# A new order for the steps of a three-stage kernel, and one PSUM bank in place of two for block 0

## The chip, the cores and the metric

The kernel runs on one core of a Trainium2 chip. The metric is device time in microseconds (us). The kernel before takes 833.93 us, the median of three runs (833.71 to 834.21).

The engines are named as in the profile: PE is TensorE's matmul, PEld its weight load, DVE is VectorE, ACT is ScalarE, POOL is GpSimd, SP is SyncE, which issues most of the transfers. A suffix q (SPq) means the engine's instruction queue.

## The reference, cut to what matters

```python
kv  = einsum('bhsd,bhse->bhde', k, v)          # 4 batches, 8 heads, 576 positions, 64 wide
a   = einsum('bhsd,bhde->bhse', q, kv)
a   = a / sqrt(mean(a * a) + 1e-06) * g_norm
x   = a as (2304 tokens, 512)
xn  = x / sqrt(mean(x * x) + 1e-06) * rms_g
x   = (silu(xn @ w_gate) * (xn @ w_val)) @ w_out     # 512 -> 1536 -> 512
h   = x @ w_in2                                      # 512 -> 2048
out = where(h > 0, h, exp(min(h, 0)) - 1) @ w_out2   # 2048 -> 512
```

All in float32. The kernel keeps every operand of a product as a high and a low part and adds three matmuls for each product (high by high, high by low, low by high).

## The kernel before

The 2304 tokens are 18 tiles of 128. The tiles are five blocks: block 0 has 256 tokens, blocks 1 to 4 have 512. Block 0 is worked alone; blocks 1 and 2, and blocks 3 and 4, are pairs (`PAIRS`).

There are three stages. The attention makes the tokens and their norm and turns them to the layout of the products. Stage 0 is the gated feed-forward (12 slices of 128 hidden columns: gate weights g, value weights v, output weights o). Stage 1 is the ELU feed-forward (16 slices, weights i and p). The output of each group of slices is added up in memory by transfers with addition (`mid`, `out`), and the last group is added on chip.

For pairs of blocks, two products with four quarters each are made from seven products instead of eight (`paired` for the hidden layer, `back_halved` for some of the output products). Each of these units opens accumulators a, b and c. Accumulator a is copied out by ACT between products ("snap"), b and c are added to the copies by DVE ("total").

Block 0 goes through `plain_hidden`. For one slice of stage 0 it makes four chunks of three 128x256 matmuls for the gate, then four for the value. After the gate's last chunk ACT computes Silu of the gate (step "gate", L933), and after the value's last chunk DVE multiplies it by the value (step "gated", L937). In the kernel before, gate and value have a PSUM bank each, of kind "g" (four banks: bg0, bg1, bg2, bo4; the first two slices use "g0", bg0 to bg2). The gate's bank is free again after "gate", the value's after "gated".

Nothing of the order is written out by hand. Every step is added to a `Plan` with an engine, an estimated length, a rank, the steps it must follow, and the buffers it takes. `Plan.run` then:

- makes an order with `order()`: at each point it takes the step that can start first, and among those that can start within 0.03 us of each other on an engine the one with the lowest rank. This pass also decides which buffer each step gets.
- makes six more passes with `again()`, whose ranks are the latest start times that `latest()` derives from the pass before; the buffers stay those of the first pass.
- keeps the pass with the earliest planned end and emits the instructions in its order. Each engine runs its own instructions in that order, one behind the other, and so does SP's queue.

The ranks that are given are multiples of 100 from one unit to the next (`R`, with `LEAD` 400 and `LEAD2` 250 for the weights); inside a unit they go by single steps, and the output products stand at 50 behind their unit.

While the keys and values are summed (until the last tile's sum), `run` puts matmuls without use (`keep_warm`, L351) where the plan shows PE idle for longer than 0.375 us. They write columns 256 to 383 of the bank whose columns 0 to 255 hold the sums of keys by values. ACT copies these sums out (`keep_kv`, L378). The loads (`LOADS`) are a chain, each behind the one before it.

Of the kernel before, what the change touches and what calls it, by code (L numbers as in the profile page):

```python
# [16 lines left out]
P = 128  # L17
D = 64
G = 2
EPS = 1e-06  # L20
WARM = 16
INF_FIELD = 2.0**-96 * 1.75


class Plan:
# [199 lines left out]
BACK_HALVED = {(0, 2): 1, (0, 4): 3, (0, 6): 3, (0, 8): 3, (1, 2): 3, (1, 4): 1, (1, 6): 3, (1, 8): 1, (1, 10): 3, (1, 12): 3}  # L225
WHOLE_AFTER = 17
SEEDS = ()
SPARE = [f"{x}{f}" for f in range(2, 12) for x in "gvo"] + [f"{x}{f}" for f in range(2, 16) for x in "ip"]


@with_exitstack
def linear_attention__swiglu__elu_kernel(
# [410 lines left out]
    def half_product(unit, X, one, two, m, c):  # L643
        _, b, a, x, first = next(p for p in PRODUCTS if p[0] == m)
        if first and c == 0:
            pbank[unit, b] = bank((unit, b))
# [9 lines left out]
    def paired(unit, X, one, two, rank, erank, xdeps, finish):  # L656
# [3 lines left out]
        U = "UZ" if unit[1:3] == (0, F1 - 1) else "U"  # L660
        snaps = {1: 1, 6: 2, 5: 4}
        before = {6: [(unit, "snap", 1)], 5: [(unit, "snap", 2)], 3: [(unit, "snap", 4)], 4: [(unit, "total", 4)]}
        for o, (m, b, a, x, first) in enumerate(PRODUCTS):
            for c in range(2):
# [3 lines left out]
                    ([(unit, m, 0)] if c else before.get(m, [])) + wdeps[a] + xdeps[x][c],  # L668
                    [("g", (unit, b))] if first and c == 0 else [],
                )  # L670
# [9 lines left out]
        for m, j in snaps.items():  # L680
            plan.add((unit, "snap", j), "ACT", AP_, erank, lambda m=m: snap(m), [(unit, m, 1)], [(U, (unit, "u", j))])
        for j, b, m in ((1, "b", 2), (4, "c", 7), (2, "c", 4)):
# [3 lines left out]
        plan.frees((unit, "b"), [(unit, "total", 1)])  # L686
        plan.frees((unit, "c"), [(unit, "total", 2)])
# [5 lines left out]
    def split_steps(ph, f, t, erank, src, after, frees):  # L693

        n = cols[t]
        key = ("act", ph, f, t)

        def high():
            if t:
                acts[ph, f, t] = tuple(place((*key, x), F32R) for x in range(2))  # L700
            else:
                a = place((*key, 0), F32R)
                acts[ph, f, t] = a[:, :n], a[:, n:2 * n]
            nc.scalar.activation(acts[ph, f, t][0], src(), AF.Copy)  # L704

        def low():
            h, l = acts[ph, f, t]
# [3 lines left out]
        keys = [(*key, x) for x in range(2 if t else 1)]  # L711
        plan.add(("ah", ph, f, t), "ACT", act_len(n, False), erank, high, after, [(kind, part) for part in keys])
# [3 lines left out]
        for part in keys:  # L716
            plan.frees(part, [(x, ph, f, t, e) for x, e in back_names(ph, f, t)])

# [70 lines left out]
    def back(k, t, rank, erank, es=None):  # L789
# [9 lines left out]
        for e in [j for _, j in back_names(ph, fs[0], t)] if es is None else es:  # L799
# [9 lines left out]
            for f in fs:  # L809
                w = "op"[ph] + str(fs[-1])  # L810
                after = [("al", ph, x, t) for x in fs] + [(w, DONE)] + turns.get(t, []) + ([("seed", t, e)] if seeded(ph, k, t) else [])
                room_ = room if f == fs[0] and not seeded(ph, k, t) else []
# [90 lines left out]
    def plain_hidden(ph, f, t, rank, erank, xdeps):  # L903
# [15 lines left out]
        prev = []  # L919
        for kind in kinds:  # L920
            for c in range(KD):
                plan.add(
                    ("hid", kind, ph, f, t, c), "PE", mm, rank + c + 10 * (kind == "v"), lambda kind=kind, c=c: chunk(kind, c),
                    [(f"{kind}{f}", DONE), *xdeps[c], *prev], [("g0" if lone else "g", ("hid", kind, ph, f, t))] if c == 0 else [],
                )
                prev = [("hid", kind, ph, f, t, c)]
        U = "U0" if lone else "U"
        if ph == 0:
            key = ("sa", f, t)

            def gate():
                s = live[key] = place(key)[:, :n]
                nc.scalar.activation(s, pbank["hid", "g", 0, f, t], AF.Silu)  # L933

            def gated():
                s = live[key]
                nc.vector.tensor_tensor(s, s, pbank["hid", "v", 0, f, t], op=ALU.mult)  # L937

            plan.add(("gate", f, t), "ACT", act_len(n, True), erank, gate, [("hid", "g", 0, f, t, KD - 1)], [(U, key)])
            plan.add(("gated", f, t), "DVE", dve(n), erank, gated, [("gate", f, t), ("hid", "v", 0, f, t, KD - 1)])  # L940
            plan.frees(("hid", "g", 0, f, t), [("gate", f, t)])
            plan.frees(("hid", "v", 0, f, t), [("gated", f, t)])
            split_steps(0, f, t, erank, lambda: live[key], [("gated", f, t)], [key])
        else:
            bkey = ("hid", "i", 1, f, t)
            elu_steps(f, t, erank, lambda: pbank[bkey], True, [(*bkey, KD - 1)], [bkey])

    def elu_steps(f, t, erank, src, psum, after, frees):

        n = cols[t]  # L950
        key = ("e", f, t)

        def relu():
            e = live[key] = place(key)[:, :n]
            nc.scalar.activation(e, src(), AF.Relu, scale=-1.0)

# [3 lines left out]
        def choose():  # L960
            nc.vector.scalar_tensor_tensor(live[key], live[key], -1.0, src(), op0=ALU.add, op1=ALU.max)  # L961

# [9 lines left out]
    def paired_gates(X, f, rank, erank, xdeps):  # L972
# [3 lines left out]
        def finish():  # L976
# [3 lines left out]
            def silu(j):  # L980
                nc.scalar.activation(u(j), u(j), AF.Silu)

# [6 lines left out]

            plan.add((unit, "silu", 1), "ACT", AS, erank, lambda: silu(1), [(unit, "total", 1)])  # L990
            plan.add((unit, "silu", 2), "ACT", AP_, erank, gate2, [(unit, 3, 1)], [("UZ" if f == F1 - 1 else "U", skey)])
# [12 lines left out]
    def paired_elus(X, fs, rank, erank, xdeps):  # L1004
# [3 lines left out]
        def finish():  # L1008
            for j, f, t in ((1, fs[0], X[0]), (4, fs[1], X[1]), (2, fs[1], X[0])):
                elu_steps(f, t, erank, lambda j=j: live[unit, j], False, [(unit, "total", j)], [(unit, "u", j)])  # L1010
# [5 lines left out]
    def back_halved(k, X, rank):  # L1016
# [57 lines left out]
        def product(m, c):  # L1074
            _, b, a, x, first = next(p for p in PRODUCTS if p[0] == m)
            key = (unit, b, c)
            if first:
                pbank[key] = bank(key)
# [5 lines left out]

        for o, (m, b, a, x, first) in enumerate(PRODUCTS):
            for c in range(2):
                plan.add(
                    (unit, m, c), "PE", 0.68, rank + o + 0.5 * c, lambda m=m, c=c: product(m, c),
                    [(unit, "l", x), *wdeps[a]] + ([(unit, before[m], c)] if m in before else []),
                    [("o", (unit, b, c))] if first else [],  # L1090
                )
        where_ = {1: (0, 0), 2: (1, 0), 4: (1, 1), 0: (0, 1)}
        for c in range(2):
# [9 lines left out]

            for m, j in ((1, 1), (6, 2), (5, 4), (3, 0)):
                plan.add((unit, f"snap{j}", c), "ACT", AP_, rank, lambda j=j, copy=copy: copy(j), [(unit, m, c)], [("P", keys[j])])
            for j, b, m in ((1, "b", 2), (4, "c", 7), (2, "c", 4)):
                plan.add((unit, f"total{j}", c), "DVE", EW, rank, lambda j=j, b=b, total=total: total(j, b), [(unit, f"snap{j}", c), (unit, m, c)])
# [3 lines left out]
            for j, key in keys.items():  # L1111
                _, _, t, e = key
                plan.add(
                    ("issue", k, t, e), "POOL", 0.95, rank,
# [423 lines left out]
```

## Time and profile before

| | |
|---|---|
| median of 3 runs | 833.93 us (833.71 to 834.21) |
| the profiled execution | 833.38 us |
| its span, first to last instruction | 831.6 us |
| outside the span | 1.8 us |
| PE busy | 822.2 us, 99% of the span, 4298 matmuls |
| DVE, ACT, POOL busy | 750.3, 604.2, 221.4 us (90%, 73%, 27%) |
| granted clock | 0.999 |

The span is what the engines do; the execution's own time is 1.8 us more. Busy times of PE overlap from one matmul to the next: a 128x512 matmul is on record for 389 ns, while one starts every 227 ns. A late matmul shows as idle time only for what is longer than this overlap. The time lost at PE is thus read from start to start.

### The profile page before, as it was taken

Reading aid. Unit: us, or ns where it says so; the run is one execution under the profiler, and the core shown is the slowest. Engines: PE = TensorE matmul, PEld = TensorE weight load, DVE = VectorE, ACT = ScalarE, POOL = GpSimd, SP = SyncE. Lnnn points to the kernel's source line nnn. Section 1 sums busy time; section 2 is a strip of 40 time slices with the busy share of each in tenths; the row PEclk is TensorE's granted clock in tenths of the full one; section 3 lists DMA queues with packets and bytes.
Section 4 is the critical chain, followed back from the end, with each engine's and each line's share of the span. In section 5 each row is a group of like instructions: output and inputs, shape, how many; then the busy total and the mean of one; then the engine's idle time right before and its main releaser. Section 6 shows DMA issues by size and latency. Waiting matters only on the chain.

```text
span 831.6 us, 12611 instructions
## 1 busy us (share of the span) xinstructions
PE 822.2 (99%) x4298; PEld 689.7 (83%) x4298; DVE 750.3 (90%) x1385; ACT 604.2 (73%) x1158; POOL 221.4 (27%) x250
## 2 busy tenths in 40 slices
PE   8999999999999999999999999999999999999998
PEld 7888878888888888888888888888888888888886
DVE  4899999998877999879899998999989998999985
ACT  2788868677656676766645778888888888798860
POOL 2556223024122204303300000043433244333230
PEclk9999999999999999999999999999999999999999
DMA  9853479249548719929853244488989599888887
GB/s 359 353 195 110 90 139 172 82 91 192 126 71 136 146 51 158 152 46 155 160 166 102 89 142 167 109 141 146 159 167 163 90 158 190 147 152 143 198 176 278
DMA packets 57296, 126.16 MB, mean 152 GB/s; under 512 B 6288, under 2 KB 10128, under 8 KB 57232
## 3 DMA queue, kind: packets, MB, share of 16 engines
q0 software_dynamic: 29792, 51.92, 42.9%
q1 hardware_dynamic: 27440, 73.45, 25.6%
q8 instruction: 33, 0.54, 0.3%
q14 instruction: 31, 0.25, 0.1%
HBM read 59.28 MB, written 66.06 MB: 151 GB/s over the span
## 4 chain that ended last, share of the span: by engine, by line
PE 92%; DVE 3%; DMA 3%; ACT 1%; issue 1%; SPq 1%; ACTq 0%
PE b L765 17%; PE hid_v L917 4%; PE hid_g L917 4%; PE hid_i L917 2%; PE b L750 2%; PE po L402 2%; DMA raw_v<-in_w_val 1%; PE pt L457 1%; DMA raw_g<-in_w_gate 1%; PE ('pb', 8, 3)_a L1083 1%; PE ('pu', 1, 6, 3)_a L651 1%; PE kv L366 1%; PE ('pb', 4, 1)_a L1083 1%; PE ('pb', 4, 3)_a L1083 1%; PE ('pu', 0, 3, 1)_a L651 1%; PE ('pu', 0, 5, 3)_a L651 1%
## 5 line engine op out<-in xcount | busy, mean ns | idle before, releaser
L1115 POOL DMA_DIRECT2D out<-part x80 | 70.2, 956 | 261.2 <-DVE part L1102 212.2
L1115 POOL DMA_DIRECT2D mid<-part x56 | 49.3, 960 | 190.7 <-DVE part L1102 146.7
L832 ACT ACTIVATE part<-b 128x512 f32<-128x512 f32 x98 | 57.2, 596 | 8.5 <-DMA mid<-part 4.5
L765 PE MATMUL b<-act,h_p 128*128 128x512 f32 x192 | 59.2, 390 | 0.0
L765 PE MATMUL b<-act,h_o 128*128 128x512 f32 x160 | 50.4, 394 | 0.7 <-ACT act L704 0.5
L838 POOL DMA_DIRECT2D mid<-part x34 | 33.8, 1048 | 53.7 <-ACT part L832 49.1
L958 ACT ACTIVATE e<-e 128x512 f32<-128x512 f32 (+1 forms) x80 | 46.2, 591 | 0.6
L765 PEld LDWEIGHTS b<-act,h_p 128*128 128x128 f32 x192 | 35.9, 188 | 7.3
L765 PE MATMUL b<-act,l_p 128*128 128x512 f32 x96 | 37.4, 389 | 0.0
L765 PEld LDWEIGHTS b<-act,h_o 128*128 128x128 f32 x160 | 29.4, 188 | 7.8 <-DVE act L708 1.0
L422 POOL TENSOR_TENSOR ri<-ms,nhalf 128x8 f32<-128x8 f32 x18 | 31.4, 1758 | 9.3 <-DVE ms L418 9.3
L838 POOL DMA_DIRECT2D out<-part x28 | 24.3, 892 | 32.0 <-ACT part L832 31.8
L765 PE MATMUL b<-act,l_o 128*128 128x512 f32 x80 | 31.2, 390 | 0.0
L891 DVE TENSOR_TENSOR far<-far,b 128x512 f32<-128x512 f32 x35 | 23.6, 681 | 5.1 <-PE b L765 3.7
L1048 DVE TENSOR_TENSOR e<-e,e 128x512 f32<-128x512 f32 x40 | 27.3, 683 | 0.2
L704 ACT ACTIVATE act<-e 128x512 fp32r<-128x512 f32 (+1 forms) x40 | 21.7, 548 | 6.8 <-DVE e L961 4.3
L917 PE MATMUL hid_g<-xh,h_g 128*128 128x256 f32 (+1 forms) x80 | 26.6, 332 | 0.0
L917 PE MATMUL hid_v<-xh,h_v 128*128 128x256 f32 (+1 forms) x80 | 26.3, 329 | 0.0
L917 PE MATMUL hid_g<-xl,h_g 128*128 128x256 f32 (+1 forms) x80 | 26.1, 326 | 0.0
L917 PE MATMUL hid_v<-xh,l_v 128*128 128x256 f32 (+1 forms) x80 | 26.1, 326 | 0.0
L917 PE MATMUL hid_g<-xh,l_g 128*128 128x256 f32 (+1 forms) x80 | 26.1, 326 | 0.0
L917 PE MATMUL hid_v<-xl,h_v 128*128 128x256 f32 (+1 forms) x80 | 26.0, 325 | 0.0
(2166 smaller groups left out, 3001.9 us busy)
## 6 DMA issues: line engine op xcount, KB each, us to landing
out<-part POOLq DMA_DIRECT2D x108, 256.0 KB, 5.6
mid<-part POOLq DMA_DIRECT2D x90, 256.0 KB, 5.4
raw_i<-in_w_in SPq DMA_DIRECT2D x16, 512.0 KB, 5.2
raw_p<-in_w_out SPq DMA_DIRECT2D x16, 512.0 KB, 4.1
raw_g<-in_w_gate SPq DMA_DIRECT2D x12, 512.0 KB, 4.3
raw_v<-in_w_val SPq DMA_DIRECT2D x12, 512.0 KB, 4.2
raw_o<-in_w_out SPq DMA_DIRECT2D x12, 512.0 KB, 5.2
mid<-part SPq DMA_DIRECT2D x18, 256.0 KB, 2.4
```

Of the source, the lines that this page charges most:

```text
L422: nc.gpsimd.tensor_tensor(ri, ms_t.pop(i), nhalf, op=ALU.pow)
L651: nc.tensor.matmul(pbank[unit, b], l[:, sl], r, start=first and c == 0 and i == 0, stop=c == 1 and i == 2, skip_group_check=True,)
L704: nc.scalar.activation(acts[ph, f, t][0], src(), AF.Copy)
L765: nc.tensor.matmul(po, l, r, start=first and i == 0 and not half, stop=f == fs[-1] and i == 2, skip_group_check=seeded(ph, k, t) or half i ...
L832: nc.scalar.activation(x, pbank["b", k, t, e][:, :n], AF.Copy)
L838: nc.gpsimd.dma_start(out=where(ph, t, e), in_=flat(live.pop(key), t or ph), accum_op=ALU.add)
L891: nc.vector.tensor_tensor(x, x, pbank["b", k, t, e][:, :n], op=ALU.add)
L917: nc.tensor.matmul(pbank[key], l, r, start=c == 0 and i == 0, stop=c == KD - 1 and i == 2)
L958: nc.scalar.activation(live[key], live[key], AF.Exp, scale=-1.0)
L1048: nc.vector.tensor_tensor(raw(*into), raw(*x), raw(*y), op=ALU.subtract)
L1083: nc.tensor.matmul(pbank[key], l[:, sl], r, start=first and i == 0, stop=i == 2, skip_group_check=True)
L1115: lambda key=key, t=t, e=e: nc.gpsimd.dma_start(out=where(ph, t, e), in_=live.pop(key), accum_op=ALU.add),
```

## The change

1. `moved(unit, move)` draws a number from a checksum of the move's number and the unit's name: in one of 4, 16 or 64 units (by the move) it is between plus and minus 4, 12, 40 or 120 (by the move), elsewhere 0. Before the first pass, every step's rank gets the sum over the 40 moves in `MOVES`. The unit is the first four parts of the step's name, or its first part where that is a tuple, so that the steps of one unit move together. The six later passes and the choice among the seven are as before.
2. For block 0 in stage 0, gate and value share one bank: the gate has columns 0 to 255, the value 256 to 511. Only the first chunk of the gate takes a bank, and the bank is free after "gated". In stage 1 block 0 keeps one bank for a slice.
3. A group's output products now name both slices' output weights as what they follow, not the last one alone.
4. Several options are added that are set so that they do nothing (`MERGED = 0`, all of `SEEDED` false, a direct store for a first group that isn't halved here), and `BACK_HALVED` has the same entries in another order.

```diff
+def moved(unit, move):
+    h = crc32(f"{move}:{unit}".encode())
+    if h % (4, 16, 64)[move // 4 % 3]:
+        return 0.0
+    return ((h >> 8) % 2001 - 1000) / 1000.0 * (4, 12, 40, 120)[move % 4]
...
     def run(self):
...
+        for n, s in self.steps.items():
+            unit = str(n[0] if isinstance(n[0], tuple) else n[:4]).replace(" ", "")
+            s["rank"] += sum(moved(unit, m) for m in MOVES)
         end = self.order()
...
+MOVES = (
+    65659, 51246, 64466, 4158, 96959, 33265, 96202, 56521, 42242, 97998, 75061, 9972, 51570, 76873,
+    91537, 40465, 99682, 83099, 22126, 67056, 32701, 42382, 27040, 37830, 75431, 40246, 15484, 54221,
+    54682, 72348, 17409, 74012, 68344, 38277, 35636, 18717, 1072, 19256, 88029, 23493,
+)
...
     def back(k, t, rank, erank, es=None):
...
-                w = "op"[ph] + str(fs[-1])
-                after = [("al", ph, x, t) for x in fs] + [(w, DONE)] + turns.get(t, []) + ...
+                after = [("al", ph, x, t) for x in (...)] + [("op"[ph] + str(x), DONE) for x in fs] + turns.get(t, []) + ...
...
     def plain_hidden(ph, f, t, rank, erank, xdeps):
...
+        one = f - f % G if ph and f < MERGED else f
+        both = ("hid", ph, one, t)
+        key_of = {k: ("hid", k, ph, f, t) if t else both for k in kinds}
+
         def chunk(kind, c):
-            key = ("hid", kind, ph, f, t)
-            if c == 0:
-                pbank[key] = bank(key)[:, :n]
+            key = key_of[kind]
+            opens = c == 0 and (t or kind == kinds[0] and f == one)
+            if opens:
+                pbank[key] = bank(key)
+            j = 0 if t else f - one if ph else int(kind == "v")
...
-                nc.tensor.matmul(pbank[key], l, r, start=c == 0 and i == 0, stop=c == KD - 1 and i == 2)
+                nc.tensor.matmul(
+                    pbank[key][:, j * n:(j + 1) * n], l, r, start=bool(opens) and i == 0, stop=c == KD - 1 and i == 2,
+                    skip_group_check=not t,
+                )
...
-                    [(f"{kind}{f}", DONE), *xdeps[c], *prev], [("g0" if lone else "g", ("hid", kind, ph, f, t))] if c == 0 else [],
+                    [(f"{kind}{f}", DONE), *xdeps[c], *prev], [("g0" if lone else "g", key_of[kind])] if opens else [],
...
-                nc.scalar.activation(s, pbank["hid", "g", 0, f, t], AF.Silu)
+                nc.scalar.activation(s, pbank[key_of["g"]][:, :n], AF.Silu)
...
-                nc.vector.tensor_tensor(s, s, pbank["hid", "v", 0, f, t], op=ALU.mult)
+                nc.vector.tensor_tensor(s, s, pbank[key_of["v"]][:, W - n:], op=ALU.mult)
...
-            plan.frees(("hid", "g", 0, f, t), [("gate", f, t)])
-            plan.frees(("hid", "v", 0, f, t), [("gated", f, t)])
+            plan.frees(key_of["g"], [("gate", f, t)])
+            plan.frees(key_of["v"], [("gated", f, t)])
```

## Rows read from the trace of the kernel before

**Rows 1.** The page: busy time of PE and DVE, and the granted clock in 40 slices

```profile
PE 822.2 (99%) x4298; PEld 689.7 (83%) x4298; DVE 750.3 (90%) x1385; ACT 604.2 (73%) x1158; POOL 221.4 (27%) x250
...
PEclk9999999999999999999999999999999999999999
```

**Rows 2.** The chain that ended last: PE's pace in stretches without a wait (start, length, what)

```profile
483.49 10.88 PE b L765 x48
```

**Rows 3.** Busy time by stretch: us, PE, PEld, DVE, ACT, POOL, clock, DMA share, GB/s

```profile
20.00:25.00 5.00, 3.75 (x61) 3.18 (x58) 4.97 (x10) 3.44 (x9) 5.00 (x5) 1.00 1.02 406
...
800.00:832.00 32.00, 27.64 (x128) 22.76 (x126) 20.37 (x34) 8.08 (x16) 2.63 (x3) 0.97 0.86 262
```

**Rows 4.** Waits of PE: who waited, for whom, us in total, times, longest

```profile
PE b L765 <- ACT act L704: 0.5, 1, 0.5
PE ('pu', 1, 0, 1)_c L651 <- ACT s L985: 0.4, 1, 0.4
PE ('pb', 13, 3)_a L1083 <- ACT part L1098: 0.3, 1, 0.3
PE b L765 <- DVE act L708: 0.2, 1, 0.2
```

**Rows 5.** Timeline of PE at the longest stall of the feed-forward

```profile
112.62 0.39 PE L917 MATMUL hid_v<-xh,l_v 128*128 128x512 f32 x1
113.49 0.50 PE L765 MATMUL b<-act,h_o 128*128 128x512 f32 x1 [0.48 <-ACT act L704]
114.22 0.50 PE L765 MATMUL b<-act,h_o 128*128 128x512 f32 x1 [0.22 <-DVE act L708]
114.56 0.40 PE L765 MATMUL b<-act,l_o 128*128 128x512 f32 x1
```

**Rows 6.** Timeline of PE at the first and last late matmuls without idle time

```profile
121.65 0.90 PE L765 MATMUL b<-act,h_o 128*128 128x512 f32 x2
122.38 0.40 PE L765 MATMUL b<-act,l_o 128*128 128x512 f32 x1
...
453.24 0.39 PE L651 MATMUL ('pu', 1, 0, 1)_a<-xh,l_i 128*128 128x512 f32 x1
453.65 0.50 PE L651 MATMUL ('pu', 0, 11, 3)_a<-xh,Sh_g 128*128 128x512 f32 x1
453.98 0.39 PE L651 MATMUL ('pu', 0, 11, 3)_a<-xl,Sh_g 128*128 128x512 f32 x1
```

**Rows 7.** The chain that ended last, just ahead of that stall

```profile
106.25 0.61 ACT part L832
...
106.88 5.34 DMA mid<-part
```

**Rows 8.** The matmuls without use: all of them by line, then one burst's timeline

```profile
L351 PE MATMUL kv<-ident x46: 275/275/378, 6.5 to 25.3; 128*128 128x128 f32 x46
...
24.21 1.38 PE L351 MATMUL kv<-ident 128*128 128x128 f32 x10 [1.25 <-ACT kv L378]
25.52 1.25 PE L402 MATMUL po<-kv,wacc 128*64 128x128 f32 x13
```

**Rows 9.** Timeline of ACT in the same stretch

```profile
23.40 0.75 ACT L378 ACTIVATE kv<-kv 64x256 f32<-64x256 f32 x2
```

**Rows 10.** Timeline of PE and ACT: block 0's slices 0 and 11

```profile
34.23 0.28 PE L917 MATMUL hid_v<-xh,h_v 128*128 128x256 f32 x1
...
34.43 0.38 ACT L933 ACTIVATE sa<-hid_g 128x256 f32<-128x256 f32 x1 [0.43 <-PE hid_g L917]
...
34.59 0.28 PE L917 MATMUL hid_v<-xh,h_v 128*128 128x256 f32 x1
...
430.06 0.28 PE L917 MATMUL hid_v<-xh,h_v 128*128 128x256 f32 x1
...
430.26 0.38 ACT L933 ACTIVATE sa<-hid_g 128x256 f32<-128x256 f32 x1
...
430.42 0.28 PE L917 MATMUL hid_v<-xh,h_v 128*128 128x256 f32 x1
```

More of the change, by code (lines that the diff above doesn't have):

```diff
@@ L22 @@
 INF_FIELD = 2.0**-96 * 1.75
+from zlib import crc32
+def moved(unit, move):
[3 more added lines that the diff above has]
+    return ((h >> 8) % 2001 - 1000) / 1000.0 * (4, 12, 40, 120)[move % 4]
 class Plan:
@@ L221, in run @@
                 call()
+MOVES = (
[3 rows of a table added]
+)
 PAIRED_FROM = (2, 2)
-BACK_HALVED = {(0, 2): 1, (0, 4): 3, (0, 6): 3, (0, 8): 3, (1, 2): 3, (1, 4): 1, (1, 6): 3, (1, 8): 1, (1, 10): 3, (1, 12): 3}
+BACK_HALVED = {(0, 2): 1, (1, 4): 1, (1, 8): 1, (0, 4): 3, (0, 6): 3, (0, 8): 3, (1, 2): 3, (1, 6): 3, (1, 10): 3, (1, 12): 3}
 WHOLE_AFTER = 17
 SEEDS = ()
+MERGED = 0
+SEEDED = {"pu0": False, "pu1": False, "pb0": False, "pb1": False}
+SEED_ORDER = (1, 7, 6, 2, 5, 3, 4)
 SPARE = [f"{x}{f}" for f in range(2, 12) for x in "gvo"] + [f"{x}{f}" for f in range(2, 16) for x in "ip"]
@@ L644, in half_product @@
         _, b, a, x, first = next(p for p in PRODUCTS if p[0] == m)
+        first = first and not (m == 2 and SEEDED[f"pu{unit[1]}"])
         if first and c == 0:
@@ L660, in paired, with seed @@
         U = "UZ" if unit[1:3] == (0, F1 - 1) else "U"
-        snaps = {1: 1, 6: 2, 5: 4}
+        seeded_ = SEEDED[f"pu{unit[1]}"]
+        snaps = {6: 2, 5: 4} if seeded_ else {1: 1, 6: 2, 5: 4}
         before = {6: [(unit, "snap", 1)], 5: [(unit, "snap", 2)], 3: [(unit, "snap", 4)], 4: [(unit, "total", 4)]}
-        for o, (m, b, a, x, first) in enumerate(PRODUCTS):
+        if seeded_:
+            before[2] = before[6]
+            def seed():
+                pbank[unit, "b"] = bank((unit, "b"))
+                nc.scalar.activation(pbank[unit, "b"], pbank[unit, "a"], AF.Copy)
+            plan.add((unit, "snap", 1), "ACT", AP_, erank, seed, [(unit, 1, 1)])
+        order = [next(p for p in PRODUCTS if p[0] == m) for m in SEED_ORDER] if seeded_ else PRODUCTS
+        for o, (m, b, a, x, first) in enumerate(order):
+            first = first and not (m == 2 and seeded_)
             for c in range(2):
@@ L668, in paired @@
                     ([(unit, m, 0)] if c else before.get(m, [])) + wdeps[a] + xdeps[x][c],
-                    [("g", (unit, b))] if first and c == 0 else [],
+                    [("g", (unit, y)) for y in ("ab" if m == 1 and seeded_ else b)] if first and c == 0 else [],
                 )
@@ L681, in paired @@
             plan.add((unit, "snap", j), "ACT", AP_, erank, lambda m=m: snap(m), [(unit, m, 1)], [(U, (unit, "u", j))])
-        for j, b, m in ((1, "b", 2), (4, "c", 7), (2, "c", 4)):
+        for j, b, m in ((1, "b", 2), (4, "c", 7), (2, "c", 4))[int(seeded_):]:
             plan.add(
@@ L685, in paired @@
             )
-        plan.frees((unit, "b"), [(unit, "total", 1)])
+        if not seeded_:
+            plan.frees((unit, "b"), [(unit, "total", 1)])
         plan.frees((unit, "c"), [(unit, "total", 2)])
@@ L693, in split_steps @@
     def split_steps(ph, f, t, erank, src, after, frees):
-        n = cols[t]
+        whole = t or ph and f < MERGED
+        n = W if whole else cols[t]
         key = ("act", ph, f, t)
+        fs = range(f, f + G) if whole and not t else [f]
         def high():
-            if t:
-                acts[ph, f, t] = tuple(place((*key, x), F32R) for x in range(2))
+            if whole:
+                both = tuple(place((*key, x), F32R) for x in range(2))
             else:
                 a = place((*key, 0), F32R)
-                acts[ph, f, t] = a[:, :n], a[:, n:2 * n]
-            nc.scalar.activation(acts[ph, f, t][0], src(), AF.Copy)
+                both = a[:, :n], a[:, n:2 * n]
+            for j, x in enumerate(fs):
+                acts[ph, x, t] = tuple(y[:, j * cols[t]:(j + 1) * cols[t]] for y in both)
+            nc.scalar.activation(both[0], src(), AF.Copy)
+            live[key] = both
         def low():
-            h, l = acts[ph, f, t]
+            h, l = live.pop(key)
             nc.vector.tensor_tensor(l, src(), h.bitcast(F32), op=ALU.subtract)
         kind = "A0" if ph == 0 and f < LONE else "A" if t else "A1"
-        keys = [(*key, x) for x in range(2 if t else 1)]
+        keys = [(*key, x) for x in range(2 if whole else 1)]
         plan.add(("ah", ph, f, t), "ACT", act_len(n, False), erank, high, after, [(kind, part) for part in keys])
@@ L716, in split_steps @@
         for part in keys:
-            plan.frees(part, [(x, ph, f, t, e) for x, e in back_names(ph, f, t)])
+            plan.frees(part, [(x, ph, f_, t, e) for f_ in fs for x, e in back_names(ph, f, t)])
     lone_f = list(range(LONE))
@@ L809, in back @@
             for f in fs:
-                w = "op"[ph] + str(fs[-1])
-                after = [("al", ph, x, t) for x in fs] + [(w, DONE)] + turns.get(t, []) + ([("seed", t, e)] if seeded(ph, k, t) else [])
+                after = [("al", ph, x, t) for x in (fs[:1] if ph and not t and fs[0] < MERGED else fs)] + [("op"[ph] + str(x), DONE) for x in fs] + turns.get(t, []) + ([("seed", t, e)] if seeded(ph, k, t) else [])
                 room_ = room if f == fs[0] and not seeded(ph, k, t) else []
@@ L916, in chunk @@
             for i, (l, r) in enumerate(((wh[:, s], mh), (wh[:, s], ml), (wl[:, s], mh))):
-                nc.tensor.matmul(pbank[key], l, r, start=c == 0 and i == 0, stop=c == KD - 1 and i == 2)
-        prev = []
+                nc.tensor.matmul(
+                    pbank[key][:, j * n:(j + 1) * n], l, r, start=bool(opens) and i == 0, stop=c == KD - 1 and i == 2,
+                    skip_group_check=not t,
+                )
+        prev = [("hid", "i", 1, one, 0, KD - 1)] if f > one else []
         for kind in kinds:
             for c in range(KD):
+                opens = c == 0 and (t or kind == kinds[0] and f == one)
                 plan.add(
                     ("hid", kind, ph, f, t, c), "PE", mm, rank + c + 10 * (kind == "v"), lambda kind=kind, c=c: chunk(kind, c),
-                    [(f"{kind}{f}", DONE), *xdeps[c], *prev], [("g0" if lone else "g", ("hid", kind, ph, f, t))] if c == 0 else [],
+                    [(f"{kind}{f}", DONE), *xdeps[c], *prev], [("g0" if lone else "g", key_of[kind])] if opens else [],
                 )
@@ L954, in relu @@
             e = live[key] = place(key)[:, :n]
-            nc.scalar.activation(e, src(), AF.Relu, scale=-1.0)
+            nc.scalar.activation(e, src()[:, :n], AF.Relu, scale=-1.0)
         def expo():
@@ L980, in silu @@
             def silu(j):
-                nc.scalar.activation(u(j), u(j), AF.Silu)
+                if SEEDED["pu0"]:
+                    live[unit, j] = place((unit, "u", j))
+                nc.scalar.activation(u(j), pbank[unit, "b"] if SEEDED["pu0"] else u(j), AF.Silu)
             def gate2():
@@ L988, in mult @@
                 nc.vector.tensor_tensor(u(j), u(j), s(), op=ALU.mult)
-            plan.add((unit, "silu", 1), "ACT", AS, erank, lambda: silu(1), [(unit, "total", 1)])
+            if SEEDED["pu0"]:
+                plan.add((unit, "silu", 1), "ACT", AP_, erank, lambda: silu(1), [(unit, 2, 1)], [("UZ" if f == F1 - 1 else "U", (unit, "u", 1))])
+                plan.frees((unit, "b"), [(unit, "silu", 1)])
+            else:
+                plan.add((unit, "silu", 1), "ACT", AS, erank, lambda: silu(1), [(unit, "total", 1)])
             plan.add((unit, "silu", 2), "ACT", AP_, erank, gate2, [(unit, 3, 1)], [("UZ" if f == F1 - 1 else "U", skey)])
@@ L1008, in finish @@
         def finish():
-            for j, f, t in ((1, fs[0], X[0]), (4, fs[1], X[1]), (2, fs[1], X[0])):
+            if SEEDED["pu1"]:
+                elu_steps(fs[0], X[0], erank, lambda: pbank[unit, "b"], True, [(unit, 2, 1)], [(unit, "b")])
+            for j, f, t in ((1, fs[0], X[0]), (4, fs[1], X[1]), (2, fs[1], X[0]))[int(SEEDED["pu1"]):]:
                 elu_steps(f, t, erank, lambda j=j: live[unit, j], False, [(unit, "total", j)], [(unit, "u", j)])
@@ L1076, in product @@
             key = (unit, b, c)
+            first = first and not (m == 2 and seeded_)
             if first:
@@ L1083, in product @@
                 nc.tensor.matmul(pbank[key], l[:, sl], r, start=first and i == 0, stop=i == 2, skip_group_check=True)
-        for o, (m, b, a, x, first) in enumerate(PRODUCTS):
+        seeded_ = SEEDED[f"pb{ph}"]
+        order = [next(p for p in PRODUCTS if p[0] == m) for m in SEED_ORDER] if seeded_ else PRODUCTS
+        if seeded_:
+            before[2] = before[6]
+        for o, (m, b, a, x, first) in enumerate(order):
+            first = first and not (m == 2 and seeded_)
             for c in range(2):
@@ L1089, in back_halved @@
                     [(unit, "l", x), *wdeps[a]] + ([(unit, before[m], c)] if m in before else []),
-                    [("o", (unit, b, c))] if first else [],
+                    [("o", (unit, y, c)) for y in ("ab" if m == 1 and seeded_ else b)] if first else [],
                 )
@@ L1102, in total, with seed, taken @@
                 nc.vector.tensor_tensor(x, x, pbank[unit, b, c], op=ALU.add)
-            for m, j in ((1, 1), (6, 2), (5, 4), (3, 0)):
+            if seeded_:
+                def seed(c=c):
+                    pbank[unit, "b", c] = bank((unit, "b", c))
+                    nc.scalar.activation(pbank[unit, "b", c], pbank[unit, "a", c], AF.Copy)
+                def taken(c=c, keys=keys):
+                    x = live[keys[1]] = place(keys[1])
+                    nc.scalar.activation(x, pbank[unit, "b", c], AF.Copy)
+                plan.add((unit, "snap1", c), "ACT", AP_, rank, seed, [(unit, 1, c)])
+                plan.add((unit, "total1", c), "ACT", AP_, rank, taken, [(unit, 2, c)], [("P", keys[1])])
+            for m, j in ((1, 1), (6, 2), (5, 4), (3, 0))[int(seeded_):]:
                 plan.add((unit, f"snap{j}", c), "ACT", AP_, rank, lambda j=j, copy=copy: copy(j), [(unit, m, c)], [("P", keys[j])])
-            for j, b, m in ((1, "b", 2), (4, "c", 7), (2, "c", 4)):
+            for j, b, m in ((1, "b", 2), (4, "c", 7), (2, "c", 4))[int(seeded_):]:
                 plan.add((unit, f"total{j}", c), "DVE", EW, rank, lambda j=j, b=b, total=total: total(j, b), [(unit, f"snap{j}", c), (unit, m, c)])
@@ L1112, in back_halved @@
                 _, _, t, e = key
+                if k == 0 or groups[k - 1][0] != ph:
+                    plan.add(
+                        ("landed", k, t, e), "DMA", 0.64, rank,
+                        lambda key=key, t=t, e=e: nc.sync.dma_start(out=where(ph, t, e), in_=live.pop(key)),
+                        [(unit, f"total{j}", c) if j else (unit, "snap0", c)], lat=2.0,
+                    )
+                    plan.frees(key, [("landed", k, t, e)])
+                    continue
                 plan.add(
```

8 lines of the change are left out of this document (4 added, 4 removed).

## The prediction

> **What bounds the kernel now.** I read the page first. PE is on record as busy for 822.2 of 831.6 us, and its granted clock is at the full level (2.4 GHz) in every slice [rows 1]. The reader should not take the 99% as it stands, since matmuls overlap on record. The second view is the chain that ended last: in a stretch without a wait 48 matmuls of 128x512 take 10.88 us, so one starts every 227 ns [rows 2]. The chain is PE for almost all of its length after the first 30 us, so PE's order of work and what it waits for set the time; DVE with 90% is the next engine.
>
> So the question is what PE loses. Its idle time is 831.6 - 822.2 = 9.4 us. The stretches say where: in 800 to 832 PE is busy for 27.64 us, and with the span's end at 831.6 some 4.0 us are the tail after the last matmul (the last sums and stores) [rows 3]. In 20 to 25 us it is idle for 1.25 us [rows 3]. Four waits in the feed-forward make 0.5 + 0.4 + 0.3 + 0.2 = 1.4 us [rows 4]. The remaining 2.7 us lie in the first 20 us, while the first data land.
>
> A wait costs more than its idle time. At the longest stall four matmuls start at 112.62, 113.49, 114.22 and 114.56: 1.94 us for three steps that take 0.68, so 1.26 us lost, of which 0.70 is on record as idle. Two waits thus cost 0.28 us each beyond their idle time [rows 5]. The other two of the four waits then cost 0.4 + 0.28 and 0.3 + 0.28. There are four more places where matmuls start late with no idle time on record. At the first, two matmuls take 122.38 - 121.65 = 0.73 us in place of 0.45; at the last, two steps take 453.98 - 453.24 = 0.74 [rows 6]. That is about 0.28 each. Together the feed-forward loses 1.26 + 0.68 + 0.58 + 4 x 0.28 = 3.6 us. This, 0.4% of the time, is all that a better order can win there. What is late at the longest stall is a copy by ACT that found its buffer still in use: the transfer into mid from it took 5.34 us, and the high part that PE waited for stood behind that copy on ACT [rows 7].
>
> **The change part by part.** *The work.* No matmul, ACT or DVE operation is added or removed, only the 46 matmuls without use can become fewer. The draws are summed when the program is built and cost nothing on the chip.
>
> *The draws.* Of the 40 moves 12 hit one unit in 4, 11 one in 16 and 17 one in 64: 12/4 + 11/16 + 17/64, so 4 draws that aren't zero for a unit on average. With their sizes the sum spreads by about 33 ranks (the root of the sum of chance x size squared / 3), where units stand 100 apart and output products 50 behind theirs. That is enough to swap neighbours, to move a weight's conversion steps among each other and to give buffers to other steps, and not enough to move a slice past the next but one. The new order is then passed six times through ranks that don't know of the draws. Gains and losses can come from each place where PE starts late, and from new ones. Bounds in the feed-forward: 3.6 us won if all eight places go; on the other side new ones of the kind seen, 0.28 to 1.26 us each. I take 3.0 us won, since each of the eight hangs on one late step that a swap of neighbours frees, and some 0.6 us are lost again elsewhere.
>
> *The start.* The 46 matmuls without use are on record until 25.3 us [rows 8]. Ten of them run from 24.21 to 25.52, so 0.13 us each with their edges. The loads are a chain whose order no rank changes, and in 20 to 25 us the transfer engines are busy throughout (share 1.02) [rows 3]. So work that waits for data can't come earlier, and only the last burst and the idle time ahead of it, 1.31 + 1.25 = 2.6 us, could be filled, with turned tiles or the first gate products. Bounds: 0 and 2.6 won, and 1 lost if the norm's chain comes later. I take 1.0 won.
>
> *One bank for gate and value.* What it saves is the second bank of kind "g" while value follows gate. PE's waits are not put down to a bank's release in that stretch, so by itself I count this at nothing; it is one of the freedoms behind the 3.0 us. What it can cost: the first burst shows a matmul that waits for ACT in the same bank. It starts at 24.21, its idle time is put down to ACT's copy L378 [rows 8], and that copy ends at 23.40 + 0.75 = 24.15 [rows 9]. The matmul writes columns 256 to 383 and the copy reads 0 to 255, so they share nothing but the bank. In the change gate and value stand in just this way. In slice 0 the value's first chunk starts at 34.23, Silu of the gate at 34.43 for 0.38 us, and the value's second chunk at 34.59 [rows 10]. In one bank Silu would wait for the first chunk's last matmul (34.23 + 0.24 + 0.28 = 34.75), and the second chunk for Silu: with 0.06 us from an end to the next start, as at 24.15, Silu runs from 34.81 to 35.19 and the chunk starts at 35.25 in place of 34.59. That is 0.65 us for one slice, and everything behind it on PE's queue moves back by as much. Who waits is then PE itself, for ACT. Five of the twelve slices stand like this before, the first and the last of them in the rows [rows 10]; in the others other products lie between, or Silu comes ahead of all value chunks or behind them. Bounds: no slice, 0; all twelve, 7.8 us lost. The nearest rows say five, 3.3 us. I take half of that, 1.6, as a stall of PE is time in which the late steps of the other places catch up, and as value chunks that need no bank of their own can be used between other products.
>
> The rows show one such wait. The Trainium skill, page "PSUM — Partial Sum Buffer", section "PSUM bank collisions raise a hardware error", says that two engines must not be in one bank and the same 32 partitions at once, disjoint columns included, and that the guard should go by bank and not by address. This speaks against the change, and the trace agrees with its one wait. By it the wait comes wherever Silu falls between two value chunks, and by columns alone it would cost nothing.
>
> *What they follow.* Naming both output weights changes nothing: conversions are a chain, so the earlier weight is done when the later one is. The options that are switched off cost nothing.
>
> *The sum.* The profiled execution took 833.38 us (span 831.6 and 1.8 around it). 833.38 - 3.0 - 1.0 + 1.6 = 831.0. The median of the runs is 0.55 above the profiled execution, so the forecast is 831.5 us, 0.3% less than before. What a measurement of this kernel can tell from no change I set at 0.2%, or 1.7 us: under 832.3 is faster and over 835.6 slower.
>
> **The rivals.** *The losses only move.* Each pass only sees planned lengths, while the late steps of the rows hang on one transfer of 5.34 us [rows 7] and on single late copies. If the same number of places is hit in the new order, the order wins 0.5 to 1.5 us, and the shared bank takes 1.6 back. The time is 833 to 835, and the likeliest 833.9. For this: what is to be won is only 0.4%, and after six passes with the same rule much of the draws may be washed out. Against it: the buffers stay those of the first pass, which the draws do change.
>
> *The shared bank decides (slower).* Value chunks that need no second bank follow the gate at once in most slices, and Silu falls between them. With nine slices 9 x 0.65 = 5.9 us are lost; with 4.0 won by the order the time is 833.9 + 1.9 = 835.8, and with half of that won 837.8. I put this case at 836.5. It decides from about six slices on: 3.9 us lost, as much as the order can be expected to win. For it: the wait is in the trace, and the five slices as well. Against it: in seven of the twelve slices the order before would lose nothing.
>
> *A transfer in the way (slower).* Transfers with addition, or SP's queue, get an order in which a fetch or a free buffer comes late. The one place of this kind cost 1.26 us [rows 5, 7]; three more make 3.8, so 836 to 837. Against it: in 700 us of feed-forward there was one.
>
> **How the numbers follow.** Forecast (831.5, from 828 to 832.3): 0.48. The losses only move: 0.30. The shared bank decides: 0.15. A transfer: 0.07. The low end is all of the 3.6 and 2.6 won with no wait in the bank, 833.9 - 6.2 = 827.7; I take 828.0. The high end, 836.0, takes in the case of the bank up to its middle. What is left out is some 0.15 above and little below. Faster: the forecast and the edge of the second case, 0.49. Within 0.2%: 0.29. Slower: both slower cases, 0.22. The forecast's own range is 828.0 to 832.3.
>
> **What the changed kernel's profile would show.** If the order wins: PE's idle time outside the first 25 us and the tail under 0.7 us (1.4 before), and fewer than eight places with late starts. If the start wins: fewer than 46 matmuls at the line of the matmuls without use, or their last one ahead of 25.3 us. If the shared bank costs: a wait of PE's value chunks for ACT's Silu in the list of waits, 0.4 to 0.7 us each, and Silu starting after the end of a value chunk. If none of the twelve shows it, that term is wrong and the time should be near 830. The prediction is wrong if waits in the shared bank stand at six slices or more, if a new wait for a transfer of over 2 us reaches PE, or if late starts are as many as before.

## The result, and the profile after

| | before | changed |
|---|---|---|
| median | 833.86 us (833.71 to 834.21, 4 runs) | 842.53 us (841.47 to 844.51, 4 runs) |
| ratio to before, 95% interval | | 1.0099 (1.0086 to 1.0112) |
| profiled execution, its span | 833.38, 831.6 us | 842.07, 840.3 us |

The changed kernel is slower by 1.0%, outside the range of the prediction. Its time also varies more from run to run: 3.0 us, against 0.5.

The work is the same. On the page PE has as many matmuls as before [rows 1]:

```profile
PE 824.1 (98%) x4298; PEld 690.2 (82%) x4298; DVE 750.1 (89%) x1385; ACT 605.2 (72%) x1158; POOL 223.0 (27%) x250
```

So the difference is in what PE waits for. The waits of PE in the changed kernel (who, for whom, us in total, times, longest), those of the start left out:

```profile
PE b L805 <- DVE far L930: 3.7, 3, 1.8
PE hid L962 <- ACT sa L982: 3.0, 6, 0.5
...
PE b L805 <- ACT part L871: 1.4, 2, 1.0
...
PE ('pu', 0, 2, 1)_c L674 <- DVE Sl_g L622: 0.4, 1, 0.4
```

Before, the feed-forward had four waits of 1.4 us [rows 4]. Now there are twelve, 8.5 us. From start to start each costs some 0.27 us more than its idle time, as before: 8.5 + 12 x 0.27 = 11.7 us, and one late start without idle time makes it 12.0. Before it was 3.6. The difference, 8.4 us, is nearly the whole of the span's 8.7.

Two groups are new. The second row is block 0's value chunks that wait for Silu of the gate. The timeline of PE and ACT in slice 0, which answers to [rows 10]:

```profile
35.09 0.28 PE L962 MATMUL hid<-xh,l_v 128*128 128x256 f32 x1
35.41 0.38 ACT L982 ACTIVATE sa<-hid 128x256 f32<-128x256 f32 x1 [0.49 <-PE hid L962]
...
35.84 0.38 PE L962 MATMUL hid<-xh,h_v 128*128 128x256 f32 x1 [0.47 <-ACT sa L982]
36.07 0.28 PE L962 MATMUL hid<-xl,h_v 128*128 128x256 f32 x1
```

Silu starts when the value's first chunk has ended (35.09 + 0.28), and the second chunk when Silu has ended (35.41 + 0.38). PE's steps of 0.12 us become 0.75 and 0.23. That is 0.74 us, or 0.8 with the longer waits of three other slices: 6 slices, 4.6 us.

The first row is mostly at the end. The chain that ended last there (start, length, what):

```profile
816.57 0.69 DVE far L930
817.25 0.61 DVE ('pu', 1, 14, 3)_u L712
817.86 3.05 DMA out<-far
...
820.96 3.48 DMA far<-out
...
824.57 0.70 DVE far L930
...
825.31 1.69 PE b L805 x6
...
827.11 0.70 DVE far L930
...
827.86 8.55 PE b L805 x42
```

PE's timeline has the two waits that stand in this chain:

```profile
825.31 0.74 PE L805 MATMUL b<-act,h_p 128*128 128x512 f32 x2 [1.84 <-DVE far L930]
...
827.86 0.73 PE L805 MATMUL b<-act,h_p 128*128 128x512 f32 x2 [0.88 <-DVE far L930]
```

Read the chain upward: PE waits for an accumulator, which DVE frees with the last addition (L930). That addition waits for the partial sums to be fetched from memory, and this fetch for a store: the fetch's buffer still holds an earlier finished sum that is on its way out. The two waits cost 1.84 + 0.88 + 2 x 0.27 = 3.3 us. Before, PE ran through its last 13.7 us without a wait:

```profile
813.92 13.73 PE b L765 x66
```

### The profile page after: what moved, and what is told of

Its sections match the earlier page's. It is cut to its first block, busy times and chain, and to the rows that moved or that the text cites. A ratio compares the mean times of both kernels' runs of the same rounds, so it can differ in the third digit from the quotient of the medians.

```text
span 840.3 us, 12585 instructions
## 1 busy us (share of the span) xinstructions
PE 824.1 (98%) x4298; PEld 690.2 (82%) x4298; DVE 750.1 (89%) x1385; ACT 605.2 (72%) x1158; POOL 223.0 (27%) x250
## 4 chain that ended last, share of the span: by engine, by line
PE 84%; DVE 8%; DMA 3%; ACT 2%; issue 1%; SPq 1%; POOL 0%; DVEq 0%; ACTq 0%; POOLq 0%
PE b L805 13%; PE hid L962 6%; PE po L424 2%; PE b L790 2%; DMA wacc<-in_q 1%; PE hid_g L962 1%; DMA raw_i<-in_w_in 1%; DVE T L1229 1%; PE pt L479 1%; PE ('pu', 1, 0, 3)_a L674 1%; PE ('pb', 12, 1)_a L1141 1%; PE ('pb', 5, 3)_a L1141 1%; PE ('pb', 13, 3)_a L1141 1%; PE kv L388 1%; PE ('pu', 0, 5, 1)_a L674 1%
## 5 line engine op out<-in xcount | busy, mean ns | idle before, releaser
L930 DVE TENSOR_TENSOR far<-far,b 128x512 f32<-128x512 f32 x35 | 23.6, 683 | 11.4 <-PE b L805 7.5
L805 PE MATMUL b<-h_p,act 128*128 128x512 f32 (+1 forms) x68 | 22.6, 378 | 0.0
L748 DVE TENSOR_TENSOR act<-e,act 128x512 fp32r<-128x512 f32 (+1 forms) x40 | 22.4, 577 | 0.2 <-ACT act L743 0.2
L805 PEld LDWEIGHTS b<-act,l_p 128*128 128x128 f32 x96 | 18.0, 188 | 3.8
L962 PE MATMUL hid<-xh,l_i 128*128 128x256 f32 x64 | 18.1, 283 | 0.0
L962 PE MATMUL hid<-xl,h_i 128*128 128x256 f32 x64 | 18.1, 283 | 0.0
L489 DVE SCALAR_TENSOR_TENSOR xl<-pt,gains_sb,xh 128x256 fp32r<-128x256 f32 x36 | 15.4, 477 | 2.9 <-ACT xh L491 2.9
```

Source lines behind the costliest of these rows:

```text
L805: nc.tensor.matmul(po, l, r, start=first and i == 0 and not half, stop=f == fs[-1] and i == 2, skip_group_check=seeded(ph, k, t) or half i ...
L930: nc.vector.tensor_tensor(x, x, pbank["b", k, t, e][:, :n], op=ALU.add)
L962: nc.tensor.matmul(pbank[key][:, j * n:(j + 1) * n], l, r, start=bool(opens) and i == 0, stop=c == KD - 1 and i == 2, skip_group_check=not t,)
```

## The experiments

Each ratio is taken to the kernel before as measured beside that run; its medians lie between 833.86 and 834.36 us, so times of different experiments compare to some 0.5 us.

The first three separate the two parts. Planned anew with one part alone, PE's order stays nearly the same as in the kernel it is compared with (by the traces some 30 of 4298 matmuls stand elsewhere with the bank alone, some 140 with the draws alone), so this separation is clean.

**The shared bank in the order before.** Same order, same buffers; nine slices put the value into the second half of the gate's bank.

```diff
+SHARE = (0, 4, 5, 6, 7, 8, 9, 10, 11)
...
+            shared = ph == 0 and not t and kind == "v" and f in SHARE
...
+            elif c == 0:
+                pbank[key] = pbank["whole", "g", f, t][:, n:2 * n]
...
```

> The kernel before with its order and its buffers to the letter, and the value of slices 0 and 4 to 11 put into the second half of the gate's bank, which the plan leaves free there. Theory of the shared bank: waits in slices 0, 4, 7, 9 and 11, where Silu is emitted between value chunks that follow each other, none in 5, 6, 8 and 10; 5 x 0.74 us, so 837.6 us. Rival, that sharing costs only with the new order: 834.

Measured: 837.95 us, 1.0047 times before (1.0035 to 1.0059). The waits of PE have a large new row:

```profile
PE hid_g L922 <- ACT sa L940: 2.4, 5, 0.5
```

Five waits, and they stand at 35, 212, 302, 369 and 435 us, in slices 0, 4, 7, 9 and 11. None stands in 5, 6, 8 or 10. 2.4 + 5 x 0.27 = 3.75 us at PE; the median rose by 4.0. The rest of PE's late places hardly changed in sum: PE now waits 0.4 us for a copy near 207 us, and two late starts of 0.3 us are gone.

**The shared bank without draws**, planned anew.

```diff
-MOVES = (65659, 51246, ...)
+MOVES = ()
```

> The shared bank without any draw, planned anew; the planned order of PE is nearly that of the kernel before, and Silu is placed between value chunks that follow each other in slices 0, 4, 7, 9 and 11. Theory of the shared bank: five waits of 0.65 to 0.8 us, so 833.9 + 3.7 = 837.6 us. Rival, that the shared bank costs nothing by itself: 834.

Measured: 837.82 us, 1.0044 (1.0032 to 1.0056). The waits of PE again have one new row:

```profile
PE hid L958 <- ACT sa L978: 2.4, 5, 0.5
```

The shared bank by itself costs 3.9 us. This run keeps everything else of the change but the draws, and the run above has the bank alone; they differ by 0.1 us. So the naming of both output weights, the new entry order and the options that are switched off cost nothing that can be measured here.

**The draws without the shared bank**, planned anew.

```diff
-        key_of = {k: ("hid", k, ph, f, t) if t else both for k in kinds}
+        key_of = {k: ("hid", k, ph, f, t) if t or ph == 0 else both for k in kinds}
...
```

> The draws with a bank each for gate and value, planned anew; the planned order of PE is nearly that of the changed kernel. Theory of the shared bank: the draws alone still lose what the tail and the start lost (3.3 and 0.6 us), so 837.5 to 839, slower than before by 0.5%. Rival, that the draws are a gain that only the bank takes back: 833 or less.

Measured: 838.86 us, 1.0062 (1.0048 to 1.0077). The draws alone cost 4.9 us, and 3.9 + 4.9 = 8.8 is nearly what the change cost, 8.7. Three of its six runs have a mean granted clock of 0.996 or 0.997; the other three have a median of 838.08, 4.2 us over before. Its chain that ended last, at the end:

```profile
802.32 0.69 DVE far L930
803.02 10.97 DMA out<-far
...
814.48 3.18 DMA out<-far
817.72 3.52 DMA far<-out
...
821.36 0.70 DVE far L930
```

The first store of a finished sum takes 10.97 us, the next fetch into its buffer can't be issued earlier, and on SP's queue the later stores and fetches stand behind it.

**Own banks for six values**, in the changed kernel's order.

```diff
+OWN = {0: "bo4", 3: "bo0", 4: "bg1", 6: "bg2", 9: "bg2", 11: "bg1"}
...
+            if alone and c == 0:
+                pbank["own", f] = ps.tile([P, 512], F32, tag=OWN[f], name=f"own_{f}")
...
```

> The changed kernel's order to the letter, but in the six slices whose value chunks waited for Silu (0, 3, 4, 6, 9, 11) the value gets a bank of its own that the plan leaves free at that time. Theory of the shared bank: the six waits are gone and their 4.6 us with them, so about 838 us, no wait of PE's value chunks for Silu in the list, and the tail's waits for the last sums as before. Rival, that the order itself is slow and the waits in the bank only stand in for others: PE waits elsewhere for the same steps, and the time stays over 841.

Measured: 840.35 us, 1.0075 (1.0061 to 1.0089), 2.2 us less than the changed kernel in place of 4.6. The waits for Silu are gone; of the others those for the late sums are as long in total as before (3.8 us, and 3.7), and those for copies have grown from 1.4 to 2.8:

```profile
PE b L806 <- DVE far L931: 3.8, 2, 2.7
PE b L806 <- ACT part L872: 2.8, 2, 2.3
```

At the end PE is idle for 2.71 us in one wait, where the changed kernel has 2.72 in two. So PE doesn't come earlier to a fixed time and wait longer there, and the rival is not borne out there. What has grown is the copy near 100 us, ahead of all but one of the repaired slices: it holds PE until 100.94 in place of 100.57, and how long it takes varies between runs. Besides, the granted clock is at half near the end of this execution (columns as in [rows 3]):

```profile
823.00:826.00 3.00, 2.62 (x6) 1.90 (x7) 2.28 (x5) 0.00 (x0) 0.00 (x0) 0.50 0.90 285
```

The clock is on record for every run. Two of the six runs have a mean of 1.000 and took 838.20 and 838.94 us; the other four, at 0.995 to 0.998, took 840.31 to 841.99. The changed kernel has three runs at 0.999 or more, with a median of 842.07. Among the runs at full clock this repair thus wins some 3.5 us of the 4.6.

**Silu behind the value's last chunk**, all else as in the changed kernel.

```diff
+LATE = (0, 3, 4, 6, 9, 11)
...
+            if self.log.index(g) < self.log.index(v):
+                self.log.remove(g)
+                self.log.insert(self.log.index(v) + 1, g)
```

> The changed kernel with the shared bank and the order of all other steps; in the six slices the Silu of the gate is emitted behind the value's last chunk, so that PE has nothing to wait for. Theory of the shared bank: as with own banks, 840.4 us, and no wait of PE for Silu. Rival, that the later Silu makes ACT or DVE late: 842 or more.

Measured: 838.57 us, 1.0050 (1.0038 to 1.0062), 4.0 us less than the changed kernel, where 840.4 was expected. No wait for Silu is left, and no new one of any size shows. The three runs at 0.999 or more have a median of 837.33, 4.7 us under those of the changed kernel: here the whole price of the bank comes back.

**Own buffers for four of the last fetches**, in the changed kernel.

```diff
+FRESH = {(3, 2): ("st0", 0), (3, 3): ("st0", 1), (4, 0): ("st1", 0), (4, 1): ("st1", 1)}
...
-                x = fetched[ph, t, e] = place(fkey)[:, :n]
+                x = fetched[ph, t, e] = fresh(fkey) if ph and (t, e) in FRESH else place(fkey)[:, :n]
...
```

> The changed kernel's order and banks; four of the last fetches of earlier sums (blocks 3 and 4) get buffers of their own, in the weight staging that is no longer used, in place of buffers whose last sum must first be stored. Theory that the new order makes the last fetches wait for stores that take 10 us: the two waits of PE near 823 and 827 us go, 3.3 us, so about 839.3 us. Rival, that the fetches are late because of the transfers with addition under way, whatever buffer they go to: the waits stay and the time is over 841.5.

Measured: 840.55 us, 1.0079 (1.0066 to 1.0092), 2.0 us less than the changed kernel where 3.3 were expected. One late wait is left at the end (0.7 us), the one near 474 us stays, and the copy near 100 us waited longer in this execution, far ahead of anything that this edit touches:

```profile
PE b L806 <- ACT part L878: 1.9, 1, 1.9
...
PE b L806 <- DVE far L937: 0.9, 1, 0.9
PE b L806 <- DVE far_st L937: 0.7, 1, 0.7
```

**Both repairs**, in the changed kernel's order.

```diff
+OWN = {0: "bo4", 3: "bo0", 4: "bg1", 6: "bg2", 9: "bg2", 11: "bg1"}
+FRESH = {(3, 2): ("st0", 0), (3, 3): ("st0", 1), (4, 0): ("st1", 0), (4, 1): ("st1", 1)}
...
```

> The changed kernel's order with both repairs: own banks for the value in six slices and own buffers for four of the last fetches. If the waits in the bank and the last fetches are the two causes: 840.35 less 3 to 4 us, 836.5 us; what is then left against the kernel before is the waits near 98, 140, 469 and 605 us. Rival, that the order loses all along its length: over 838.5.

Measured: 835.52 us, 1.0014 (1.0005 to 1.0023). The two repairs take back 7.0 of the 8.7 us. Own banks win 5.0 us where the last fetches are repaired and 2.2 where not, and own buffers 4.8 or 2.0. About half of this gap is the granted clock: none of the twelve runs here is under 0.999, and among runs at 0.999 or more own banks alone win 3.5. What makes the other half isn't shown.

**The draws with own buffers, and with four copies moved besides.** The first has separate banks, planned anew. In the second, copies near 98 to 120 us go to buffers that no transfer reads.

```diff
...
+AT = {("part", 0, 3, 3): "kvb1", ("part", 0, 3, 2): "kvb0", ("part", 0, 4, 2): "kvb1", ("part", 1, 2, 1): "kvb0"}
...
-        tag = plan.where[key]
+        tag = AT.get(key, plan.where[key])
```

> The draws with a bank each for gate and value, and own buffers for four of the last fetches. Theory that the draws' loss is the last fetches: 838.9 less 3 to 4.4 us, so 835 us. Rival, that the draws lose elsewhere too and the tail only takes its turn: over 837.

> As the run with the draws and own buffers for the last fetches, and four copies near 98 to 120 us go to the two buffers of the attention's sums, so that none waits for a transfer that still reads its buffer. Theory: the wait of PE near 98 us (1.4 us) goes as well, so 833.5 us; what the draws' order then has left to lose are the waits near 467 and 604 us. Rival: 835, as without it.

Measured: 836.77 us, 1.0042 (1.0029 to 1.0055), more than expected and just under its rival: the copies near 100 and 605 us waited 2.3 us in all in its trace, 0.6 more than in the draws alone, which hides part of the repair. And 833.58 us, 0.9996 (0.9987 to 1.0005), as expected. With the fetches and the copies repaired the order of the draws is as fast as the order before, no faster.

**The kernel before with three copies moved.** Same edit, in the kernel before.

```diff
+AT = {("part", 0, 3, 1): "kvb1", ("part", 0, 4, 1): "kvb0", ("part", 0, 4, 3): "kvb1"}
...
```

> The kernel before, order and banks to the letter; three copies near 97, 112 and 115 us go to the two buffers of the attention's sums, which are no longer used, in place of buffers that a transfer into memory still reads. Theory that a buffer still in use makes the stall at 112.6 us: 1.26 us less, 832.7 us, and the two waits of PE for act are gone. Rival, that the stall is DVE's load and comes back within some us: 833.9.

Measured: 832.46 us, 0.9982 (0.9974 to 0.9990): faster than both kernels. The waits of PE, those of the start left out:

```profile
PE ('pu', 1, 0, 1)_c L652 <- ACT s L986: 0.4, 1, 0.4
PE ('pb', 13, 3)_a L1084 <- ACT part L1099: 0.3, 1, 0.3
PE ('pu', 0, 4, 3)_a L652 <- ACT ('pu', 0, 4, 3)_u L675: 0.3, 1, 0.3
```

The two waits for act [rows 4, 5] are gone. A small one that had almost no idle time before now has 0.3 us. Like for like, with late copies moved in both orders, the order before stands at 0.9982 and that of the draws, which has its fetches repaired besides, at 0.9996; their intervals overlap by a little.

## Why the prediction was wrong

*What bounds the kernel* was right: the span went up by what PE lost from start to start. But I looked only at waits that reached PE, and counted the last 4 us as a tail that stays, and nothing ahead of it. The transfers at the end had little to spare before: the nearest fetches landed some 2 us ahead of their sums (one at 816.01, its sum at 818.07). In the changed kernel the fetch of 820.96 landed at 824.44, and its sum began at 824.57.

*The draws* are the step that failed most: "I take 3.0 us won, since each of the eight hangs on one late step that a swap of neighbours frees". Measured alone they lost 4.9 us. The swaps also change which buffer each step gets. In the new plan six of the eighteen last fetches go to a buffer whose finished sum must first be stored, where four did before. And the plan can't see what this costs: it gives such a store 0.64 us on the queue and 2.0 us to land, and in the trace of the draws alone the first one took 10.97. This was the rival "a transfer in the way", at 0.07; its price of 3.8 us was near, its place was not. The eight late places of before weren't freed either: the longest (a copy whose buffer a transfer still reads) came back near 100 us, and others came at 140, 473, 487 and 609. Without the bank and the end, these five cost 4.1 us from start to start, where the eight cost 3.6, much as the rival that the losses only move had it. Repaired at the end and at the copies, the new order equals the old one. So it held no gain to be set against its losses.

*The start*, 1.0 us won, was wrong: the matmuls without use are still 46, and the first gate product starts at 32.2 us where it started at 31.6. In all the traces it lies between 31.6 and 32.9, in either order, so this is no loss either.

*One bank* had the right mechanism and, for one slice, nearly the right size: 0.65 us predicted, 0.73 to 0.8 measured. The count was wrong. I took half of the five slices' price, as "a stall of PE is time in which the late steps of the other places catch up". In the order before five waits cost 4.0 us, all of them; the other places' late steps did not catch up. The five slices named from the rows were the right ones. The new order made them six, which the prediction had named as a sign of being wrong.

The Trainium skill, page "PSUM — Partial Sum Buffer", section "PSUM bank collisions raise a hardware error", has the guard by bank. The trace agrees: PE waited for Silu in six slices of the changed kernel, and in five of each run that shared the bank in the old order, though gate and value share no column. The list of waits is read from semaphores, so these are waits that the program holds. What would come without the guard no run here shows.

*What they follow* and the options that are switched off cost nothing that shows, as predicted: with them the shared bank costs 3.9 us and without them 4.0.

The rival of the bank (836.5) and that of the transfer (836 to 837) were priced against gains of the order. Both came true, and the gains did not; 833.9 + 3.9 + 4.9 = 842.7 is near the measured 842.5. What stays open is which of the draws moves the fetches, since they were only tried together, and why the copy near 100 us waits between 0.9 and 2.3 us in traces of the same order.

## What to carry to other kernels

Two halves of one bank, filled by PE and emptied by another engine, aren't independent in this kernel: in the trace PE waits for the reader of the other half, so count every place where the reader falls between two writes in the order of instructions, at the full price; here it was enough to put the reader behind the last write. Ahead of reordering, list the transfers that are just in time, on their queue and by the buffer that they wait for, since a plan that counts a store as 2.6 us, where one here took 11, can make them late. And a late copy whose buffer is still read by a transfer is repaired by another buffer, without touching the order.

## What the runs showed of the hardware

A finished sum stored at 803.02 in the run with the draws alone took 10.97 us; the last transfers with addition were under way then, one of them issued at 805.49. The chain shows a store of 814.48 there at 3.18. That the additions slow the store is not shown.

In the run with Silu behind the value, PE's granted clock fell at the end. Busy time by stretch (us, PE, PEld, DVE, ACT, POOL, clock, DMA share, GB/s):

```profile
818.00:823.00 5.00, 3.05 (x12) 1.82 (x11) 1.96 (x4) 0.00 (x0) 0.00 (x0) 0.97 0.94 286
823.00:826.00 3.00, 2.25 (x6) 1.78 (x6) 1.28 (x2) 0.00 (x0) 0.00 (x0) 0.50 0.96 272
826.00:829.00 3.00, 3.00 (x8) 2.33 (x8) 1.37 (x2) 0.00 (x0) 0.00 (x0) 0.50 1.03 397
```

PE had been idle for 1.95 us up to 821.30. From 823 on it ran at 0.50 (1.2 of 2.4 GHz) for six microseconds, with another idle time of 0.75 us in them: 8 matmuls on record in 3 us. The changed kernel, with idle times of 1.84 and 0.88 us at the same place, kept its clock:

```profile
829.00:832.00 3.00, 3.00 (x15) 2.48 (x14) 1.78 (x3) 0.00 (x0) 0.00 (x0) 1.00 1.04 376
```

It has 15 matmuls in 3 us. The run with the draws alone kept its clock after idle times of 2.97 and 0.87 us, and the run with own banks lost it in one of 2.71. So the length of the idle time doesn't tell these traces apart.

The mean granted clock of every run shows what this does to the times. Of the 22 runs of the four kernels that keep the late fetches (the changed one, the draws alone, own banks, Silu behind the value) eleven have 0.998 or less. Of the 55 runs of the other seven experiments four have, and of the 49 runs of the kernel before beside the experiments none. In each of the four every run at 0.998 or less took at least as long as the slowest one at 0.999 or more; with the draws alone the medians are 840.49 and 838.08. So a stall at the end costs about half of the executions twice, some 1.5 to 2.5 us more, and this is part of why the changed kernel's time varies more. Where in a run without a profile the clock fell is not on record.
